# Column order of a gated product, and split loads of a grouped attention's values

## The chip, the cores and the metric

The kernel runs on one core of one Trainium2 chip: TensorE multiplies matrices, VectorE, ScalarE and GpSimd work elementwise, SyncE issues transfers, and 16 DMA engines move data between HBM and SBUF. The metric is device time in microseconds (us) of one execution; lower is better. The profile shows one execution, and its times count from the first instruction.

## The reference

Attention of two kinds is added, and the sum, one row of 512 for each of 8 x 576 = 4608 tokens, goes through a gated product and two further matrices. The inputs are float32 (the weights arrive as 64-bit words that the kernel joins itself).

```python
B, H, S, D = 8, 8, 576, 64
q_d, k_d, v_d = (x.reshape(B, H, S // 4, 4, D).mean(axis=3) for x in (q, k, v))
out_up = np.repeat(sm_attn(q_d, k_d, v_d), 4, axis=2)          # pooled attention, 144 positions
scores = np.where(abs(pos[:, None] - pos[None, :]) < 4, scale * q @ k.T, -1e9)
out_local = softmax(scores) @ v                                # each token sees 7 neighbours
x = (out_up + out_local).transpose(0, 2, 1, 3).reshape(4608, 512)
h = ((x @ w1) * (x @ w2)) @ w3                                 # w1, w2: 512 x 1024, w3: 1024 x 1024
return h @ w_out                                               # w_out: 1024 x 512
```

## The kernel before, in words

**Units and chunks.** A batch element has three units of 192 tokens, so there are 24 units. Two units make a chunk of 384 tokens (CT), and 12 chunks, c = 0 to 11, go through the gated product one after the other. w3 and w_out are multiplied once at the start (fold, the accw products), so that a chunk needs the gates (pab) and one product with the folded matrix wphl (acc).

**Local attention** is made in two ways. The first two batch elements (PB, units 0 to 5, chunks 0 to 2) use group_unit: TensorE computes scores of groups of 16 positions, each of four tokens, against the 18 positions around them. Each unit has three groups; load_v fetches the values of 18 positions x 4 tokens as 72 rows of 2 KB into a buffer v_w, of which there are four (BUFS vw). A group that straddles position 72, where the array in HBM has its halves, is fetched in two transfers. group_values (oe_ps) consumes them. The other batch elements (units 6 to 23, chunks 3 to 11) use unit: VectorE, with ScalarE's help, multiplies and adds windows of q, k and v (q_t, kv, pr, pv, xl), with partitions (head, block), where a sequence is cut into NB = 16 blocks of BT = 36 tokens. In such a unit the token columns of x run (token in block, block), so 16 neighbouring columns are one token offset in 16 blocks.

**Pooled attention** (pooled, quad; s_ps, t_ps, o_ps) is computed once per batch element and added to x. Its v sums are made by accumulating transfers that GpSimd issues.

**The gated product.** moe(c) takes x as high and low parts (xh, xl). For each of eight blocks f of 128 features, TensorE makes both gates into PSUM (pab, 24 products of 384 columns); ScalarE copies the first gate (a, L1008); VectorE multiplies the second into it (L1010); ScalarE writes its high part gh (L1015); VectorE subtracts to the low part gl (L1017). There are two buffers each of a, gh and gl. Then TensorE multiplies 128-column slices of gh and gl, as weights, with wphl: nine products of 512 columns for each f (lines 310 to 312, in this order: gh with the high part, gh with the low part, gl with the high part). The three results (acc) are copied to o_sb, 128 tokens each, and stored by SyncE; in the last chunk the middle one is copied by VectorE and issued from ScalarE's queue. A column of gh is a row of o_sb. For chunks 0 to 2 a store is contiguous; from chunk 3 on a tile of 128 rows is 8 token offsets of 16 blocks (or 4 and 4 of two batch elements), and its rows go to HBM through out_v with the token outermost and the block inside.

**Order.** Every task belongs to an engine's queue, and the order on each queue is written out by hand (ORDER); the costs in the code only merge these queues. SyncE's queue mixes all loads and stores in one order, and a store or load that waits for data or a buffer holds what stands behind it.

Of the kernel before, what the change touches and what calls it, by code (L numbers as in the profile page):

```python
# [8 lines left out]
F32 = mybir.dt.float32  # L9
# [5 lines left out]
ALU = mybir.AluOpType  # L15
# [8 lines left out]
NB = 16  # L24
BT = S // NB
NJ = 3
# [4 lines left out]
QB = SD // 2  # L31
# [7 lines left out]
UN = UT * NB  # L39
CT = 2 * UN  # L40
# [3 lines left out]
PB = (0, 1)  # L44
GS = 16
GQ = GS * FAC
WS = GS + 2
# [140 lines left out]
class Plan:  # L188
# [14 lines left out]
    def add(self, eng, cost, fn, deps=(), take=(), uses=(), late=0.0):  # L203

        got, rings, after = [], [], []
        for r in take:
            held, old, last = r.take()
            got.append(held)
            rings.append(old)
            after += last[:1]  # L210
        t = Task(eng, cost, fn, [d for d in deps if d is not None], late, rings, after, self.group)
        for h in list(got) + list(uses):
            h.append(t)
        self.tasks.append(t)
        return (t, *got) if take else t
# [32 lines left out]
def dve_us(n, fast=False):  # L248
    return n / 1920 + 0.155 if fast else n / 960 + 0.1


def act_us(n, pointers=0, psum=False):
    return n / 1200 + (0.08 if psum else 0.1 if pointers else 0.145) + 0.093 * pointers - (0.03 if psum and pointers else 0.0)
# [6 lines left out]
def mm_us(n):  # L260
    return n * 0.43e-3 + 0.0095
# [5 lines left out]
def dma_us(n, add=False, rate=300e3):  # L267
    return n / (180e3 if add else rate)
# [3 lines left out]
def tile_attention_moe(ctx: ExitStack, tc: tile.TileContext, q, kw, vw, qk4, v4, w1, w2, w3, wout, edge, out):  # L272
    nc = tc.nc
# [32 lines left out]
    add = plan.add  # L306
    R = {k: Ring(n) for k, n in BUFS.items()}

    def three(out_ps, lh, ll, rh, rl, first, last):
        nc.tensor.matmul(out_ps, lhsT=lh, rhs=rh, start=first, stop=False)  # L310
        nc.tensor.matmul(out_ps, lhsT=lh, rhs=rl, start=False, stop=False)  # L311
        nc.tensor.matmul(out_ps, lhsT=ll, rhs=rh, start=False, stop=last)  # L312
# [371 lines left out]
    @plan.named  # L684
    def group_unit(n):
        b, j = divmod(n, NJ)
        c, u = divmod(n, 2)
        T = {}
        starts = [(GS * g, min(max(GS * g - 1, 0), SD - WS)) for g in range(NG * j, NG * j + NG)]

        T["v"], lvs, hvs = [None] * NG, [], []
        for g, (_, k0) in enumerate(starts):
            def load_v(g=g, k0=k0):
                T["v"][g] = pools["pep"].tile([GK, H * D], F32, name="v_w", bufs=BUFS["vw"])
                i = k0
                while i < k0 + WS:
                    m = min(k0 + WS, i // QB * QB + QB)
                    nc.sync.dma_start(out=T["v"][g][FAC * (i - k0):FAC * (m - k0)], in_=v4[b, :, i % QB:i % QB + m - i, i // QB].rearrange("f j h d -> j f (h d)"))
                    i = m
            lv, hv = add("SP", 0.55 * (1 + (k0 < QB < k0 + WS)), load_v, take=[R["vw"]], late=dma_us(GK * 2048))  # L700
            lvs.append(lv)
            hvs.append(hv)
        pep.extend(lvs)
        quads = [group_scores(b, j, qd, starts) for qd in range(2)]

        @plan.named
        def rest(n):
            hpt = None
            pts = []
            for qd, (U, hs, no) in enumerate(quads):  # L710
                def flip(U=U):
                    for par in range(2):
                        U["t", par] = ps.tile([GK, NG, 2 * GQ], F32, tag="g", name="te_ps", bufs=BUFS["ps"])
                        for g in range(NG):
                            nc.tensor.transpose(out=U["t", par][:, g], in_=U["p"][:, par, g], identity=ident)  # L715
                fl, *banks = add("PE", 2 * NG * 0.106, flip, no, take=[R["ps"], R["ps"]], uses=[hs])
                pep.append(fl)
                for par, bank in enumerate(banks):
                    def keep(par=par, U=U, qd=qd):
                        if qd == par == 0:  # L720
                            T["pt"] = pools["pep"].tile([GK, NQ, 2, NG, GQ], F32, name="pte", bufs=BUFS["pte"])
                        nc.scalar.copy(out=T["pt"][:, 2 * qd:2 * qd + 2, par].rearrange("p w g q -> p g w q"), in_=U["t", par].rearrange("p g (w q) -> p g w q", w=2))
                    if hpt is None:
                        th, hpt = add("ACT", act_us(UN * 2, psum=True), keep, [fl], take=[R["pte"]], uses=[bank])
                    else:
                        th = add("ACT", act_us(UN * 2, psum=True), keep, [fl, pts[0]], uses=[bank, hpt])
                    pts.append(th)
            pep.extend(pts)
            group_values(n, T, pts, hpt, lvs, hvs)
        return rest  # L730
# [225 lines left out]

    group = lambda f: 0 if f < 4 else f // 2 - 1
    per = lambda f: 4 if f < 4 else 2
    out_v = out.rearrange("(b k t) m -> b t k m", k=NB, t=BT)

    @plan.named
    def moe(c):
        T = {}
# [22 lines left out]
        for f in range(NF):  # L986
            plan.group = f"gates {c} {f}"
            ends, banks = [], []
            for which in range(2):
                t = None  # L990
                for part in range(2):
                    def mmul(which=which, part=part, f=f):
                        whl, fs = gates[which][group(f)], slice(f % per(f) * 128, f % per(f) * 128 + 128)
                        if part == 0:
                            T["p", which, f] = ps.tile([128, CT], F32, tag="ab", name="pab", bufs=BUFS["ab"])
                        for kk in (2 * part, 2 * part + 1):
                            three(T["p", which, f], whl[:, kk, 0, fs], whl[:, kk, 1, fs], chunks[c][0][:, kk], chunks[c][1][:, kk], kk == 0, kk == KT - 1)
                    d = [t] + x_ready[c] + g_ready[which, group(f)]
                    if part == 0:
                        t, bank = add("PE", 6 * mm_us(CT), mmul, d, take=[R["ab"]], uses=[x_held[c]])  # L1000
                    else:
                        t = add("PE", 6 * mm_us(CT), mmul, d, uses=[x_held[c], bank])
                ends.append(t)
                banks.append(bank)

            def copy_a(f=f):
                T["a", f] = work.tile([128, CT], F32, name="a", bufs=BUFS["a"])
                nc.scalar.copy(out=T["a", f], in_=T["p", 0, f])  # L1008
            ta, ha = add("ACT", act_us(CT, psum=True), copy_a, [ends[0]], take=[R["a"]], uses=[banks[0]])
            tg = add("DVE", dve_us(CT), lambda f=f: nc.vector.tensor_tensor(out=T["a", f], in0=T["p", 1, f], in1=T["a", f], op=ALU.mult), [ta, ends[1]], uses=[ha, banks[1]])  # L1010

            def hi(f=f):
                T["gh", f] = work.tile([128, CT], F32R, name="gh", bufs=BUFS["g"])
                T["gl", f] = work.tile([128, CT], F32R, name="gl", bufs=BUFS["g"])
                nc.scalar.copy(out=T["gh", f], in_=T["a", f])  # L1015
            th, hg = add("ACT", act_us(CT), hi, [tg], take=[R["g"]], uses=[ha])
            tl = add("DVE", dve_us(CT), lambda f=f: nc.vector.tensor_tensor(out=T["gl", f], in0=T["a", f], in1=T["gh", f].bitcast(F32), op=ALU.subtract), [th], uses=[ha, hg])  # L1017
            lag.append((f, [th, tl], hg))

        for f, d, hg in lag:  # L1020
# [13 lines left out]
        for i, (t, ho) in enumerate(kept):  # L1034
            def store(i=i):
                lo = i * 128
                queue = nc.scalar if last and i == 1 else nc.sync
                while lo < i * 128 + 128:
                    n = 2 * c + lo // UN
                    b, t = n // NJ, (n % NJ) * UT + lo % UN // NB  # L1040

                    hi = min(i * 128 + 128, lo // UN * UN + UN if b in PB else lo + (BT - t) * NB)
                    o = T["o", i][lo - i * 128:hi - i * 128]
                    if b in PB:
                        nc.sync.dma_start(out=out[c * CT + lo:c * CT + hi], in_=o)
                    else:
                        queue.dma_start(out=out_v[b, t:t + (hi - lo) // NB], in_=o)
                    lo = hi
            add("SP", 0.5, store, [t] + [k for k, _ in kept[2:] if last and i == 1], uses=[ho], late=dma_us(128 * 2048))

# [128 lines left out]
```

## Time and profile before

| | |
|---|---|
| time, median of 3 runs | 756.76 us (755.49 to 761.6) |
| the profiled execution | 758.0 us, span 756.2 us from first to last instruction |
| granted TensorE clock, mean | 0.995 of 2.4 GHz |
| busy: TensorE products | 741.5 us (98%) |
| busy: VectorE, ScalarE, GpSimd | 608.0 (80%), 534.8 (71%), 128.4 us (17%) |
| moved by DMA | 111.89 MB, mean 148 GB/s |

Busy times are shares of the whole span; what a change in one stage is worth must be read from that stage. Matmuls are pipelined, so a busy TensorE says that products follow one another, not how long one takes. Issuing a transfer is not counted as busy time.

### The profile page before, as it was taken

The numbers are of one execution on the slowest core, as the hardware profiler recorded it, in microseconds if no ns is written. First come the engines' busy times: TensorE is split into PE (matmuls) and PEld (weight loads), VectorE is DVE, ScalarE is ACT, GpSimd is POOL, SyncE is SP. The second block draws the span as 40 slices with busy tenths as digits, with TensorE's granted clock in tenths as the row PEclk, the third lists the DMA queues.
The fourth block names the chain that finished last, engine by engine and source line by source line (L and its number), as shares of the span: only waits on it lengthen the run. The fifth ranks groups of instructions, "written<-read, shape, count | busy, mean of one in ns | idle before, by whom it ended". The sixth has DMA issues, their size and how long they took to land.

```text
span 756.2 us, 14865 instructions
## 1 busy us (share of the span) xinstructions
PE 741.5 (98%) x5288; PEld 646.5 (85%) x5288; DVE 608.0 (80%) x1063; ACT 534.8 (71%) x2133; POOL 128.4 (17%) x163
## 2 busy tenths in 40 slices
PE   7999999999999999999999999999999999999995
PEld 5445798889989999999998998999989898999995
DVE  4867995649999999999899989999988897866111
ACT  4689878658987887797687786887786876762211
POOL 2120013220202321222131220223100222010000
PEclk9999999999999999999999999999999999999998
DMA  8998666646766777657865866577754556232101
GB/s 297 303 233 274 218 199 116 136 88 188 133 171 172 162 165 187 138 117 152 215 113 167 179 129 149 131 173 148 183 117 126 120 117 146 60 68 43 41 1 42
DMA packets 51462, 111.89 MB, mean 148 GB/s; under 512 B 5548, under 2 KB 19884, under 8 KB 51388
## 3 DMA queue, kind: packets, MB, share of 16 engines
q0 software_dynamic: 15360, 38.94, 30.9%
q1 hardware_dynamic: 35892, 71.75, 29.5%
q8 instruction: 41, 0.67, 0.4%
q14 instruction: 33, 0.27, 0.1%
q10 hardware_dynamic: 136, 0.26, 0.1%
HBM read 80.26 MB, written 9.44 MB: 119 GB/s over the span
## 4 chain that ended last, share of the span: by engine, by line
PE 93%; DMA 4%; DVE 1%; ACT 1%; issue 0%; SPq 0%; DVEq 0%; ACTq 0%
PE pab L310 18%; PE pab L312 18%; PE pab L311 18%; PE acc L310 9%; PE acc L311 9%; PE acc L312 9%; PE accw L414 4%; DMA raw<-in_w_dram 4%; PE o_ps L529 2%; PE t_ps L607 2%; PE s_ps L568 2%; PE oe_ps L788 1%; PE se_ps L745 1%; PE te_ps L715 1%; DMA v_w<-in_v_dram 1%
## 5 line engine op out<-in xcount | busy, mean ns | idle before, releaser
L918 ACT ACTIVATE pv<-kv,s 128x64 f32<-128x64 f32 x432 | 115.2, 338 | 14.4 <-DVE s L895 9.1
L870 ACT ACTIVATE junk<-pr 128x64 f32<-128x64 f32 x432 | 110.4, 256 | 17.3 <-DVE pr L860 7.8
L860 DVE TENSOR_TENSOR pr<-q_t,kv 128x768 f32<-128x768 f32 x126 | 116.5, 951 | 1.7 <-ACT junk L870 0.9
L310 PE MATMUL acc<-wphl,gh 128*128 128x512 f32 x288 | 114.1, 396 | 0.0
L312 PE MATMUL acc<-wphl,gl 128*128 128x512 f32 x288 | 112.9, 392 | 0.0
L311 PE MATMUL acc<-wphl,gh 128*128 128x512 f32 x288 | 112.8, 392 | 0.0
L934 POOL DMA_DIRECT2D xl<-pv x54 | 49.3, 912 | 321.2 <-DVE xl L936 263.8
L1010 DVE TENSOR_TENSOR a<-pab,a 128x384 f32<-128x384 f32 x96 | 53.0, 553 | 53.4 <-PE pab L312 52.5
L1008 ACT COPY a<-pab 128x384 f32<-128x384 f32 x96 | 45.2, 471 | 59.0 <-PE pab L312 51.8
L873 DVE TENSOR_REDUCE s<-pr 128x12 f32<-128x768 f32 x90 | 84.3, 946 | 0.3
L870 ACT ACTIVATION_READ_ACCUMULATOR junk<-pr 128x1 f32 x432 | 81.2, 188 | 0.0
L1015 ACT CAST gh<-a 128x384 fp32r<-128x384 f32 x96 | 48.4, 508 | 42.2 <-PE acc L311 29.7
L926 DVE TENSOR_TENSOR pv<-kv,s 128x768 f32<-128x768 f32 x72 | 67.8, 951 | 1.8 <-DMA xl<-pv 1.2
L310 PE MATMUL pab<-xh,wb 128*128 128x384 f32 x192 | 66.1, 344 | 0.0
L310 PE MATMUL pab<-xh,w1a 128*128 128x384 f32 x192 | 65.7, 342 | 0.0
L310 PE MATMUL pab<-xh,wo 128*128 128x384 f32 x192 | 65.3, 340 | 0.0
L312 PE MATMUL pab<-xh,wb 128*128 128x384 f32 x192 | 65.1, 339 | 0.0
L311 PE MATMUL pab<-xl,wb 128*128 128x384 f32 x192 | 65.0, 339 | 0.0
L310 PE MATMUL pab<-xh,w2a 128*128 128x384 f32 x192 | 64.9, 338 | 0.0
L312 PE MATMUL pab<-xh,wo 128*128 128x384 f32 x192 | 64.5, 336 | 0.0
L312 PE MATMUL pab<-xh,w1a 128*128 128x384 f32 x192 | 64.5, 336 | 0.0
L311 PE MATMUL pab<-xl,w1a 128*128 128x384 f32 x192 | 64.4, 336 | 0.0
(120 smaller groups left out, 1716.7 us busy)
## 6 DMA issues: line engine op xcount, KB each, us to landing
xl<-pv POOLq DMA_DIRECT2D x54, 384.0 KB, 4.3
raw<-in_w_dram SPq DMA_DIRECT2D x32, 512.0 KB
qks<-in_qk_dram POOLq DMA_DIRECT2D x18, 576.0 KB, 7.3
kv<-in_kw_dram SPq DMA_DIRECT2D x18, 576.0 KB
kv<-in_vw_dram SPq DMA_DIRECT2D x18, 576.0 KB
out_dram<-o_sb SPq DMA_DIRECT2D x29, 256.0 KB
q_t<-in_q_dram SPq DMA_DIRECT2D x18, 384.0 KB
raw<-in_wout_dram SPq DMA_DIRECT2D x8, 512.0 KB
```

Source lines behind the costliest of these rows:

```text
L310: nc.tensor.matmul(out_ps, lhsT=lh, rhs=rh, start=first, stop=False)
L311: nc.tensor.matmul(out_ps, lhsT=lh, rhs=rl, start=False, stop=False)
L312: nc.tensor.matmul(out_ps, lhsT=ll, rhs=rh, start=False, stop=last)
L860: (nc.gpsimd if o in share["qk_pool"] else nc.vector).tensor_tensor(out=T[o], in0=T["q"], in1=T["k"][:, o * D:o * D + nq].rearrange("p (t ...
L870: nc.scalar.activation(out=junk, in_=T[o][:, t], func=AF.Copy, accum_out=T["s"][:, t, o:o + 1])
L873: reds.append(add("DVE", dve_us(nq), lambda o=o: nc.vector.tensor_reduce(out=T["s"][:, :, o], in_=T[o], op=ALU.add, axis=AX.X), [tp], uses ...
L918: nc.scalar.mul(out=T["pv", o][:, tt], in_=T["v"][:, (tt + o) * D:(tt + o + 1) * D], mul=T["s"][:, tt, o:o + 1])
L926: nc.vector.tensor_tensor(out=T["pv", o], in0=T["v"][:, o * D:o * D + nq].rearrange("p (t d) -> p t d", d=D), in1=T["s"][:, :, o].unsqueez ...
L934: t = add("Pool", 0.9, lambda o=o: nc.gpsimd.dma_start(out=T["x"], in_=T["pv", o], accum_op=ALU.add), [t, tm], uses=[hx, h], late=dma_us(1 ...
L1008: nc.scalar.copy(out=T["a", f], in_=T["p", 0, f])
L1010: tg = add("DVE", dve_us(CT), lambda f=f: nc.vector.tensor_tensor(out=T["a", f], in0=T["p", 1, f], in1=T["a", f], op=ALU.mult), [ta, ends[ ...
L1015: nc.scalar.copy(out=T["gh", f], in_=T["a", f])
```

## The change

In load_v, a group's 18 positions are fetched as a transfer of 16 positions and one of 2 (16 of the 18 groups; the two that straddle the halves stay two transfers of 9). In moe, from chunk 3 on (runs_of gives 0 before), gh and gl are written with their columns turned: within each run of r tokens (r = 8, and 4 in chunks 4, 7 and 10, where a chunk holds two batch elements) the order (token, block) becomes (block, token). The copy to gh writes through the turned view, and the subtraction writes gl and reads gh through it; a is read as before. The stores follow: a run of r tokens goes to HBM with the 16 blocks outermost and its r tokens, neighbouring rows, inside. In chunks 4, 7 and 10 each tile of 128 rows holds two runs, hence two stores. Orders, buffers and costs stay the same.

```diff
--- before.py
+++ after.py
@@ -694,7 +694,7 @@
                 T["v"][g] = pools["pep"].tile([GK, H * D], F32, name="v_w", bufs=BUFS["vw"])
                 i = k0
                 while i < k0 + WS:
-                    m = min(k0 + WS, i // QB * QB + QB)
+                    m = min(k0 + WS if i > k0 else k0 + GS, i // QB * QB + QB)
                     nc.sync.dma_start(out=T["v"][g][FAC * (i - k0):FAC * (m - k0)], in_=v4[b, :, i % QB:i % QB + m - i, i // QB].rearrange("f j h d -> j f (h d)"))
                     i = m
             lv, hv = add("SP", 0.55 * (1 + (k0 < QB < k0 + WS)), load_v, take=[R["vw"]], late=dma_us(GK * 2048))
@@ -956,7 +956,20 @@
 
     group = lambda f: 0 if f < 4 else f // 2 - 1
     per = lambda f: 4 if f < 4 else 2
-    out_v = out.rearrange("(b k t) m -> b t k m", k=NB, t=BT)
+    out_v = out.rearrange("(b k t) m -> b k t m", k=NB, t=BT)
+    out_t = out.rearrange("(b k t) m -> b t k m", k=NB, t=BT)
+
+
+    def runs_of(c):
+        if any(n // NJ in PB for n in (2 * c, 2 * c + 1)):
+            return 0
+        return 8 if (2 * c + 1) % NJ else 4
+
+    def by_block(x, c, turned):
+        r = runs_of(c)
+        if not r:
+            return x
+        return x.rearrange("p (i k t) -> p i t k" if turned else "p (i t k) -> p i t k", k=NB, t=r)
 
     @plan.named
     def moe(c):
@@ -1012,9 +1025,9 @@
             def hi(f=f):
                 T["gh", f] = work.tile([128, CT], F32R, name="gh", bufs=BUFS["g"])
                 T["gl", f] = work.tile([128, CT], F32R, name="gl", bufs=BUFS["g"])
-                nc.scalar.copy(out=T["gh", f], in_=T["a", f])
+                nc.scalar.copy(out=by_block(T["gh", f], c, True), in_=by_block(T["a", f], c, False))
             th, hg = add("ACT", act_us(CT), hi, [tg], take=[R["g"]], uses=[ha])
-            tl = add("DVE", dve_us(CT), lambda f=f: nc.vector.tensor_tensor(out=T["gl", f], in0=T["a", f], in1=T["gh", f].bitcast(F32), op=ALU.subtract), [th], uses=[ha, hg])
+            tl = add("DVE", dve_us(CT), lambda f=f: nc.vector.tensor_tensor(out=by_block(T["gl", f], c, True), in0=by_block(T["a", f], c, False), in1=by_block(T["gh", f], c, True).bitcast(F32), op=ALU.subtract), [th], uses=[ha, hg])
             lag.append((f, [th, tl], hg))
 
         for f, d, hg in lag:
@@ -1038,13 +1051,14 @@
                 while lo < i * 128 + 128:
                     n = 2 * c + lo // UN
                     b, t = n // NJ, (n % NJ) * UT + lo % UN // NB
-
-                    hi = min(i * 128 + 128, lo // UN * UN + UN if b in PB else lo + (BT - t) * NB)
+                    r = runs_of(c)
+
+                    hi = min(i * 128 + 128, lo // UN * UN + UN if n // NJ in PB else lo + (r or BT - t) * NB)
                     o = T["o", i][lo - i * 128:hi - i * 128]
-                    if b in PB:
+                    if n // NJ in PB:
                         nc.sync.dma_start(out=out[c * CT + lo:c * CT + hi], in_=o)
                     else:
-                        queue.dma_start(out=out_v[b, t:t + (hi - lo) // NB], in_=o)
+                        queue.dma_start(out=out_v[b, :, t:t + r] if r else out_t[b, t:t + (hi - lo) // NB], in_=o)
                     lo = hi
             add("SP", 0.5, store, [t] + [k for k, _ in kept[2:] if last and i == 1], uses=[ho], late=dma_us(128 * 2048))
 
```

## Rows read from the trace of the kernel before

**Rows 1.** Windows: stretch, length, busy us of each engine, TensorE's clock, DMA share, GB/s.

```profile
200.00:600.00 400.00, 400.00 (x2595) 366.51 (x2594) 374.79 (x583) 314.66 (x1374) 81.14 (x95) 1.00 0.67 152
...
638.30:645.00 6.70, 6.70 (x56) 6.17 (x41) 3.32 (x5) 4.07 (x13) 0.00 (x0) 0.75 0.42 135
```

**Rows 2.** Chain that ended last, whole span: by line; a piece (start, us, what).

```profile
by line: PE pab L310 18.3%; PE pab L312 17.7%; PE pab L311 17.6%; PE acc L310 8.8%; PE acc L311 8.7%; PE acc L312 8.7%; PE accw L414 4.1%; DMA raw<-in_w_dram 3.6%; PE o_ps L529 2.0%; PE t_ps L607 1.7%; PE s_ps L568 1.7%; PE oe_ps L788 1.2%;
...
635.39 1.73 issue
```

**Rows 3.** Timeline 745 to 757: start, us, engine, line, operation [idle before, releaser].

```profile
747.75 1.97 SPq L1047 DMA_DIRECT2D out_dram<-o_sb  x2
...
748.50 0.58 ACT L1031 COPY o_sb<-acc 128x512 f32<-128x512 f32 x1 [0.77 <-PE acc L312]
748.54 1.22 ACTq L1047 DMA_DIRECT2D out_dram<-o_sb  x1
```

**Rows 4.** Windows of the last microseconds, columns as in rows 1.

```profile
749.00:750.00 1.00, 0.00 (x0) 0.00 (x0) 0.00 (x0) 0.08 (x1) 0.00 (x0) 1.00 0.54 61
750.00:751.00 1.00, 0.00 (x0) 0.00 (x0) 0.00 (x0) 0.00 (x0) 0.00 (x0) 1.00 0.44 154
...
752.00:753.00 1.00, 0.00 (x0) 0.00 (x0) 0.00 (x0) 0.00 (x0) 0.00 (x0) 0.50 0.52 197
...
754.00:755.00 1.00, 0.00 (x0) 0.00 (x0) 0.00 (x0) 0.00 (x0) 0.00 (x0) 0.50 0.09 31
```

**Rows 5.** DMA view 697 to 703, GB/s in 40 slices: one store alone.

```profile
GB/s 0 0 0 0 0 0 0 0 0 0 0 0 0 0 68 109 55 55 27 27 55 41 96 205 164 164 205 218 164 82 14 0 0 0 0 0 0 0 0 0
```

**Rows 6.** DMA view 216 to 222, GB/s in 40 slices: a contiguous store comes first.

```profile
GB/s 0 0 0 0 0 0 0 0 0 137 410 410 410 314 164 259 177 177 178 246 218 191 178 273 154 92 0 184 307 338 338 430 430 369 430 399 270 0 0 0
```

**Rows 7.** Timeline 153 to 164: v_w's last loads and the product that waits.

```profile
155.91 2.08 SPq L698 DMA_DIRECT2D v_w<-in_v_dram  x2
...
161.66 1.16 PEld L788 LDWEIGHTS oe_ps<-pte,v_w 72*32 72x32 f32 x80 [0.40 <-DMA v_w<-in_v_dram]
161.66 1.32 PE L788 MATMUL oe_ps<-pte,v_w 72*32 72x64 f32 x80 [0.24 <-DMA v_w<-in_v_dram]
```

**Rows 8.** Chain that ended last, 155 to 163: the load's piece.

```profile
156.83 4.79 DMA v_w<-in_v_dram
```

**Rows 9.** Issues of lines 698 and 1047: ns min/median/max, first and last start.

```profile
L698 SPq DMA_DIRECT2D v_w<-in_v_dram x20: 754/764/1156, 56.9 to 156.8; - x20
...
L1047 SPq DMA_DIRECT2D out_dram<-o_sb x29: 543/610/1005, 324.0 to 749.1; - x29
```

**Rows 10.** SyncE's waits: line, releaser, us in total, times, longest.

```profile
SPq L842 <- DVE pv L926: 105.4, 7, 27.7
```

**Rows 11.** Groups by form: out<-in, shapes, count | busy us, mean ns | idle before.

```profile
L1017 DVE TENSOR_TENSOR gl<-a,gh 128x384 fp32r<-128x384 f32 x96 | 52.6, 552 | 14.4 <-ACT gh L1015 14.1
...
L1015 ACT CAST gh<-a 128x384 fp32r<-128x384 f32 x96 | 48.4, 508 | 42.2 <-PE acc L311 29.7 <-DVE a L1010 9.3 <-DVE gl L1017 1.5
...
L954 DVE TENSOR_TENSOR xl<-xt,xh 128x768 fp32r<-128x768 f32 x18 | 17.1, 953 | 2.5 <-ACT xh L953 2.5
...
L342 ACT ACTIVATE w<-raw 128x512 f32<-128x512 f32 x16 | 11.1, 703 | 4.2 <-DMA raw<-in_w_dram 4.1
...
L648 DVE COPY qn<-q 128x576 f32<-128x576 f32 x8 | 5.1, 654 | 0.0
...
L467 ACT CAST w1a<-wx 128x512 fp32r<-128x512 f32 x4 | 2.5, 617 | 0.3 <-DVE wx L357 0.3
```

**Rows 12.** Timeline 693 to 697: gl of a chunk's last feature block, and its products.

```profile
695.61 0.55 DVE L1017 TENSOR_TENSOR gl<-a,gh 128x384 fp32r<-128x384 f32 x1
...
696.47 0.39 PE L310 MATMUL acc<-wphl,gh 128*128 128x512 f32 x1
...
696.92 0.39 PE L312 MATMUL acc<-wphl,gl 128*128 128x512 f32 x1
```

**Rows 13.** Timeline 589 to 592.6: a chunk's last x, and its first gate product.

```profile
590.41 0.96 DVE L954 TENSOR_TENSOR xl<-xt,xh 128x768 fp32r<-128x768 f32 x1 [0.90 <-ACT xh L953]
...
592.27 0.44 PE L310 MATMUL pab<-xh,w1a 128*128 128x384 f32 x1
```

## The prediction

> **What bounds the kernel now.** I read busy time by stage, then the chain that ended last, then the end of the timeline, then each place that the change touches. Between 200 and 600 us TensorE is busy for all of the 400 us at full clock, VectorE for 374.79 and ScalarE for 314.66 [rows 1]. The chain says the same: three lines of matmuls on two tiles, six entries, make 80% of the span [rows 2]. So a microsecond counts in two ways only: TensorE is made to wait (or stops waiting), or something lies behind its last matmul. VectorE is the next candidate: it idles 25.2 us in those 400, and what it is given more is hidden only while that lasts. One wait of TensorE is left late in the run, 1.73 us at 635.39, ahead of the pooled values' products; what it waited for the chain doesn't name [rows 2]. Behind it the granted clock is 0.75 between 638.3 and 645 [rows 1]: half of those 6.7 us at 1.2 and not 2.4 GHz, a loss of 1.7 us.
>
> The end: the last chunk's stores are issued by SyncE, the first at 747.75 and the last at 749.1, behind ScalarE's last copy (748.50, for 0.58), and by ScalarE's queue at 748.54, which takes 1.22 [rows 3, 9]. From 749 on nothing but these three stores of 256 KB moves, with a busy share of the transfer engines of 0.44 to 0.54 and, once all are under way, 154 to 197 GB/s; the last microsecond with data has 31 GB/s, 0.2 us at that rate, so data ends at 754.2 [rows 4], 2.0 us ahead of the span's end. A busy share near one half fits a store spread over eight of sixteen engines. These 5 us hold the run's only exposed stores.
>
> **Part 1, stores by block.** From chunk 3 on the token columns in gh and gl are put in the order (block, token), so that a store's slowest dimension in memory is 16 blocks and not 8 or 4 tokens. Two rows price a store of 256 KB. The one of the stretch from 697, in the old shape, moves its data in 17 slices of 0.15 us, 2.5 us, slow for the first 1.2 us and then at up to 218 GB/s [rows 5]. The first burst from 216, a contiguous store, has 137, three times 410 and 314 GB/s, 252 KB in 0.7 us [rows 6]. The new shape writes 8 neighbouring rows for each block and then jumps, so it is nearer to the second, but it may start slowly like the first. At the end the second and third store start their data at about 750.1 (the issue on ScalarE's queue ends at 749.76, and 749 to 750 has only 61 GB/s [rows 4]). Both at 410 GB/s need 1.3 us, to 751.4; at 2.5 us together, to 752.6. With the same 2.0 us behind, the end moves from 756.2 to 753.4 or 754.6: a gain of 1.6 to 2.8. I take 2.3, on the side of the contiguous row. The earlier stores are waited for by nobody on the path: cost and gain nothing. In chunks 4, 7 and 10 each tile is stored in two pieces where two of the three went in one: 6 more issues of 0.61 us [rows 9]. Behind them on SyncE stand the loads of q, k and v for VectorE's units; SyncE itself waits for buffers there (105.4 us in 7 waits at one line [rows 10]), which covers them. Without that cover: 3.6 us.
>
> **Part 2, the turned columns.** gh (ScalarE) and gl (VectorE) are written with a step of 32 bytes (16 in chunks 4, 7, 10) between neighbouring elements instead of 4, and gl's subtraction reads gh with that step too. 72 of 96 instructions of each kind change; TensorE reads both contiguously as before. Now they take 508 and 552 ns for 384 elements [rows 11]. No row has a write with such a step. The nearest are reads: VectorE's copy of 576 elements with a step of 576 bytes takes 654 [rows 11]; its slope from 384 to 768 contiguous elements is (953 - 552)/384 = 1.04 ns, so the elements alone are 599, and at a doubled price they would be near 1200. On ScalarE, 512 elements read with a step of 8 bytes take 703, contiguous ones 617 [rows 11] (the function differs too): 0.17 ns an element. So I take VectorE +0 and ScalarE +65 ns for 384 elements. Bounds: nothing, and the element time doubled, 384 x 1.04 = 400 ns on VectorE and, with the slope (617 - 508)/128 = 0.85, 327 on ScalarE. A gain is excluded: as many instructions on as many elements.
>
> [...]
>
> Where does a price go? Gates and down-products are staggered, and there is a margin from gl's end to the product that needs it. It is smallest in the last feature block of a chunk: gl starts at 695.61 and takes 0.55, the block's first product starts at 696.47, the one that reads gl 0.45 later [rows 12]. So 0.3 to 0.75 us stand against 0.065 expected, and 0.33 or 0.73 at the bounds. The other way is VectorE's pace: a chunk's last x is ready at 591.37, TensorE's first product with it starts at 592.27 [rows 13]. If VectorE loses ScalarE's 65 ns in each of 8 waits for gh, that is 0.5 us a chunk, inside these 0.9. For what gets through, mainly the wait at 635 growing, I put down 0.4 us.
>
> **Part 3, v of a group as 16 and 2 positions.** 16 of the 18 group loads become two transfers (two straddle the halves and stay two of 9). An issue takes 764 ns in the median, a store's 610 [rows 9], so 16 more cost SyncE 10 to 12 us, spread from 57 to 157 us. Behind them stand weight loads and the next v. The place that decides is the last unit: two loads are issued from 155.91 on, back to back, when TensorE has freed their buffers [rows 7]. The one at 156.83 takes 4.79 us to land [rows 8], and for it TensorE starts 0.24 late at 161.66, its weight load 0.40 [rows 7]. Four issues take the place of two, and the last 2 positions go out at about 155.91 + 3 x 0.8 = 158.3. A piece of a ninth of the size may land in 3 us, at 161.3, which ends the wait of 0.40, or in the same 4.79, at 163.1, 1.4 later than now. I take +0.2, nearer to the short end, since the piece is small.
>
> [...]
>
> **The sum.** -2.3 + 0.4 + 0.2 = -1.7. The profiled execution took 758.0 (span 756.2, and 1.8 around it), so 756.3; the median of the three runs is 1.24 lower, 756.76, so 755.1 against it.
>
> **The rivals.** (a) Writes at the doubled price on both engines. VectorE gets 72 x 0.4 = 29 us more. Chunks 3 to 9 lie in the stretch of 400 us: 56 x 0.4 = 22 us against 25.2 idle, of which I let half be usable, since the rest is waiting for matmuls, gh and transfers that stays. The 10 us left over, and 2 or 3 more from chunk 10 and from waits for a later gh, come onto TensorE through x: +12, 767, slower. It decides from about 0.2 us more per gl. For it stand VectorE's pace and the margin of 0.9; against it the 654 ns. [...] (b) ScalarE alone doubles: 24 us on an engine with 85 idle in the 400; VectorE waits longer for gh and the smallest margins break: +1 to +3, 757. (c) The last v comes 1.4 late and the clock falls behind it as at 638: 1.4 + 1.7 in place of 0.2, 758.0. (d) The stores are no faster, since memory or issue and not the number of engines sets their pace (the slow first 1.2 us of [rows 5] speak for it, the busy share of one half [rows 4] against): 757.4. (e) The wait at 635 and its clock go, because transfers ahead of it shift: -3.4, 751.7.
>
> **How the numbers follow.** The forecast (by the bounds of its terms 753.6 to 757) 0.65; (a) 0.08; (b) 0.10; (c) 0.06; (d) 0.07; (e) 0.04. 1% is 7.6 us, about what a measurement of this kernel can tell from no change (the runs lie from 755.49 to 761.6). Only (a) passes it upward; below it there is no case, and 0.02 is left for what I haven't seen: faster 0.02, same 0.90, slower 0.08. The range takes in the forecast, (b), (c) and (d) with some spread of runs, and stops at (e): 752.0 to 759.5.
>
> **What would show it.** Right: over 300 GB/s behind 749 with a busy share near 1, the last data before 753, a span near 754.5; gl at 552 ns, gh between 508 and 600; no new wait of TensorE. Wrong: gl over 750 or gh over 800 ns, and TensorE waiting for x or gl in chunks 3 to 10; a wait for v near 161 of over 1 us with a lower clock behind it; last stores still at a half share.

## The result, and the profile after

The changed kernel took 763.82 us (median of 6 runs, 763.22 to 768.29) against 757.07 for the kernel before (6 runs on the same chip, 754.68 to 761.6): ratio 1.0102 with a 95% interval of 1.0062 to 1.0141. (Ratios here and below are those on record, computed over the runs; they are not the quotient of the two medians.) That is slower by about 1%, outside the range of 752.0 to 759.5, and the wrong way from 755.1. The profiled execution took 763.33, with a span of 761.5 against 756.2.

The costliest groups by form first (columns as in [rows 11]; these lines answer to gh and gl there, 508 and 552 ns; idle is the engine's idle time before them and what ended it):

```profile
L1028 ACT CAST gh<-a 128x384 fp32r<-128x384 f32 x96 | 78.9, 829 | 35.5 <-PE acc L311 19.8 <-DVE a L1023 9.4 <-DVE pr L860 3.3
L1030 DVE TENSOR_TENSOR gl<-a,gh 128x384 fp32r<-128x384 f32 x96 | 78.7, 823 | 18.8 <-ACT gh L1028 18.3
```

Both are means over the 24 contiguous instructions of chunks 0 to 2 and the 72 turned ones. By the view of one tile, the eight gl and gh of chunk 3 (a step of 32 bytes between written elements) and then of chunk 4 (16 bytes) take, in ns, min/median/max:

```profile
L1030 DVE TENSOR_TENSOR gl<-a,gh x8: 859/960/1017, 275.8 to 320.8; 128x384 fp32r<-128x384 f32 x8
L1028 ACT CAST gh<-a x8: 929/982/1107, 274.5 to 319.8; 128x384 fp32r<-128x384 f32 x8
...
L1030 DVE TENSOR_TENSOR gl<-a,gh x8: 837/858/870, 332.5 to 373.2; 128x384 fp32r<-128x384 f32 x8
L1028 ACT CAST gh<-a x8: 866/884/891, 330.8 to 372.3; 128x384 fp32r<-128x384 f32 x8
```

The median of the 32-byte step is 408 ns over the 552 that gl took before: the "element time doubled", 400 ns, that stood in the prediction as a bound. gh has 474 more, beyond its bound of 327. Over all six chunks with this step the medians are 939 and 959 (+387 and +451), and single instructions spread from 850 to 1107.

What TensorE does with that, in the timeline of the end of chunk 5 (start, us, engine, line, operation, idle before and its releaser):

```profile
429.49 0.55 DVE L1023 TENSOR_TENSOR a<-pab,a 128x384 f32<-128x384 f32 x1
...
430.13 0.94 ACT L1028 CAST gh<-a 128x384 fp32r<-128x384 f32 x1 [1.02 <-DVE a L1023]
...
431.11 0.93 DVE L1030 TENSOR_TENSOR gl<-a,gh 128x384 fp32r<-128x384 f32 x1 [0.20 <-ACT gh L1028]
...
431.13 0.19 PEld L310 LDWEIGHTS acc<-wphl,gh 128*128 128x128 f32 x1 [0.26 <-ACT gh L1028]
...
432.09 0.19 PEld L312 LDWEIGHTS acc<-wphl,gl 128*128 128x128 f32 x1 [0.67 <-DVE gl L1030]
432.10 0.50 PE L312 MATMUL acc<-wphl,gl 128*128 128x512 f32 x1 [0.23 <-DVE gl L1030]
```

The weight load of the product with gh sat idle for 0.26 us until gh ended, that of the product with gl for 0.67 until gl ended at 432.04. The two prices lie one behind the other, a, then gh, then gl, where the last feature block of a chunk had 0.3 to 0.75 us to spare [rows 12]. The chain that ended last, by line, says it of the whole span:

```profile
by line: issue 13.7%; PE pab L310 8.8%; PE pab L312 8.4%; PE pab L311 8.4%; DVE pr L860 5.1%; PE acc L310 4.0%; PE acc L312 3.9%; PE acc L311 3.8%; PE accw L414 3.6%; DVE s L873 3.3%; DVE gl L1030 3.1%; DMA xl<-pv 2.6%; ACT junk L870 2.3%;
```

TensorE's six lines fall from 80% [rows 2] to 37%, and VectorE's own work (pr, s, gl) is in it. (The 13.7% called issue is time in which the engine waited for nothing that the profile shows.)

Waits of TensorE, and of its weight loads (us in total, times, longest); in the trace of before only one of them has a counterpart, the weight loads' wait for a, with 0.3 in one wait:

```profile
PE pab L310 <- DVE a L1023: 1.5, 4, 0.6
PE acc L312 <- DVE gl L1030: 1.2, 3, 0.7
...
PE pab L310 <- ACT a L1021: 0.8, 2, 0.5
```

```profile
PEld acc L312 <- DVE gl L1030: 4.9, 8, 1.1
...
PEld pab L310 <- DVE a L1023: 3.9, 7, 1.0
```

The weight loads tell more than the matmuls, whose modelled ends cover short delays (0.23 idle against 0.67 at 432.1 above): the idle time before the five loads that can wait here (L312 acc, and L310 for wb, wo, w1a and w2a) adds up to 19.9 us before and 30.6 after. The largest of the five, before and after (busy, mean ns, idle before):

```profile
L312 PEld LDWEIGHTS acc<-wphl,gl 128*128 128x128 f32 x288 | 54.0, 188 | 11.7
...
L312 PEld LDWEIGHTS acc<-wphl,gl 128*128 128x128 f32 x288 | 54.0, 188 | 16.3 <-DVE gl L1030 4.9
```

Besides gl itself, TensorE waits for a, which frees the gate's bank (pab) and comes late because ScalarE and VectorE do. No line names x.

The windows of the stretch of [rows 1] and of the tail (columns as there):

```profile
200.00:600.00 400.00, 396.90 (x2549) 357.67 (x2548) 383.19 (x573) 322.98 (x1348) 78.52 (x91) 1.00 0.66 150
```

```profile
756.00:757.00 1.00, 0.25 (x2) 0.00 (x0) 0.30 (x1) 0.59 (x1) 0.00 (x0) 1.00 0.26 57
757.00:758.00 1.00, 0.00 (x0) 0.00 (x0) 0.00 (x0) 0.00 (x0) 0.00 (x0) 1.00 0.83 231
758.00:759.00 1.00, 0.00 (x0) 0.00 (x0) 0.00 (x0) 0.00 (x0) 0.00 (x0) 1.00 0.88 254
759.00:760.00 1.00, 0.00 (x0) 0.00 (x0) 0.00 (x0) 0.00 (x0) 0.00 (x0) 1.00 0.78 242
```

In the same 400 us the trace has 46 products fewer than in [rows 1], 2549 and 2595 (a few records can be missing from a trace). The last stores now move 231 to 254 GB/s at a share of 0.78 to 0.88, where [rows 4] has 61 to 197 at about one half; and the last issue on ScalarE's queue takes 0.66 instead of 1.22:

```profile
755.54 1.90 SPq L1061 DMA_DIRECT2D out_dram<-o_sb  x2
...
755.86 0.39 PE L312 MATMUL acc<-wphl,gl 128*128 128x512 f32 x1
756.29 0.59 ACT L1044 COPY o_sb<-acc 128x512 f32<-128x512 f32 x1 [0.77 <-PE acc L312]
756.33 0.66 ACTq L1061 DMA_DIRECT2D out_dram<-o_sb  x1
```

The account of the span: chunk 3 starts (first product of w1a) at 267.68 instead of 269.42, -1.74; from there to the start of the last product 488.18 instead of 478.65, +9.53; from there to the end 5.64 instead of 8.13, -2.49. Sum +5.30, which is 761.5 - 756.2.

By chunk, from one chunk's first product to the next one's (us; the last to its last product's start). The three right columns are runs of the next section.

| chunk | written step | before | after | gl alone (dve_only) | gh alone (act_only) | padded_short |
|---|---|---|---|---|---|---|
| 3 | 32 bytes | 53.71 | +2.13 | +0.87 | +0.19 | +1.86 |
| 4 | 16 | 52.85 | +0.51 | +0.20 | 0.00 | +2.77 |
| 5 | 32 | 54.94 | +2.01 | +1.02 | -0.02 | +3.49 |
| 6 | 32 | 53.93 | +0.57 | +0.30 | 0.00 | +0.57 |
| 7 | 16 | 51.63 | +1.08 | +0.54 | 0.00 | +1.50 |
| 8 | 32 | 55.80 | +1.76 | +1.22 | +1.23 | +1.90 |
| 9 | 32 | 56.32 | +1.35 | +2.09 | -0.22 | +1.76 |
| 10 | 16 | 49.92 | +0.15 | +0.12 | +0.10 | +0.22 |
| 11 | 32 | 49.56 | -0.02 | -0.02 | 0.00 | 0.00 |

Chunk 9 holds the wait at 635 of the kernel before and its half clock [rows 1, 2] (0.50 from 639 to 642, where products of 384 columns start 0.32 us apart, against 0.17 or 0.18 at 699 with a clock of 1.00), and chunk 8 is 1.19 longer in split_only too, which turns nothing; copy_plain, below, which changes nothing near chunk 9, is 1.30 shorter there. These two lines are less sure. In chunks 3 to 7, which have neither, the change costs 6.30 us. The last chunk costs nothing. Each column is one profiled execution.

### The profile page after: what moved, and what is told of

Same layout as the page of the kernel before. It is cut to its first block, busy times and chain, and to the rows that moved or that the text cites. A ratio compares the mean times of both kernels' runs of the same rounds, so it can differ in the third digit from the quotient of the medians.

```text
span 761.5 us, 14897 instructions
## 1 busy us (share of the span) xinstructions
PE 746.9 (98%) x5288; PEld 644.6 (85%) x5288; DVE 632.6 (83%) x1063; ACT 558.2 (73%) x2133; POOL 128.8 (17%) x163
## 3 DMA queue, kind: packets, MB, share of 16 engines
q0 software_dynamic: 15360, 38.94, 30.6%
## 4 chain that ended last, share of the span: by engine, by line
PE 47%; DVE 22%; issue 14%; ACT 8%; DMA 6%; POOL 3%; SPq 0%; DVEq 0%; POOLq 0%; ACTq 0%
PE pab L310 9%; PE pab L312 8%; PE pab L311 8%; DVE pr L860 5%; PE acc L310 4%; PE acc L312 4%; PE acc L311 4%; PE accw L414 4%; DVE s L873 3%; DVE gl L1030 3%; DMA xl<-pv 3%; ACT junk L870 2%; DVE pv L926 2%; DVE xl L936 2%; DMA raw<-in_wout_dram 2%
## 5 line engine op out<-in xcount | busy, mean ns | idle before, releaser
L312 PE MATMUL acc<-wphl,gl 128*128 128x512 f32 x288 | 113.8, 395 | 1.5 <-DVE gl L1030 1.2
L310 PE MATMUL acc<-wphl,gh 128*128 128x512 f32 x288 | 114.3, 397 | 0.0
L1028 ACT CAST gh<-a 128x384 fp32r<-128x384 f32 x96 | 78.9, 829 | 35.5 <-PE acc L311 19.8
L1030 DVE TENSOR_TENSOR gl<-a,gh 128x384 fp32r<-128x384 f32 x96 | 78.7, 823 | 18.8 <-ACT gh L1028 18.3
L312 PEld LDWEIGHTS acc<-wphl,gl 128*128 128x128 f32 x288 | 54.0, 188 | 16.3 <-DVE gl L1030 4.9
L310 PE MATMUL pab<-xh,wb 128*128 128x384 f32 x192 | 65.8, 343 | 0.6 <-DVE a L1023 0.4
L310 PE MATMUL pab<-xh,w2a 128*128 128x384 f32 x192 | 65.3, 340 | 1.1 <-DVE a L1023 1.1
L310 PE MATMUL pab<-xh,wo 128*128 128x384 f32 x192 | 65.7, 342 | 0.6 <-ACT a L1021 0.5
L310 PE MATMUL pab<-xh,w1a 128*128 128x384 f32 x192 | 65.8, 343 | 0.0
L312 PE MATMUL pab<-xh,wb 128*128 128x384 f32 x192 | 64.6, 336 | 0.0
L312 PE MATMUL pab<-xh,wo 128*128 128x384 f32 x192 | 64.5, 336 | 0.0
```

The source lines that it names most:

```text
L1028: nc.scalar.copy(out=by_block(T["gh", f], c, True), in_=by_block(T["a", f], c, False))
```

## The experiments

The diffs are against the changed kernel, or against the kernel before where the text says "in the kernel before". Ratios are against the kernel before on the same chip.

**split_only.** Part 3 alone, in the kernel before.

```diff
-                    m = min(k0 + WS, i // QB * QB + QB)
+                    m = min(k0 + WS if i > k0 else k0 + GS, i // QB * QB + QB)
```

> Part 3 alone: v of a group as 16 and 2 positions; columns and stores as before. Theory A (the loss is the doubled time of gh's and gl's writes): gh 508 and gl 552 ns as before, no loss, and the time is 757 less what the split itself gives. Of that there are two readings: the changed kernel started chunk 2 (TensorE's first product with w1a) 1.75 us earlier than before; if the split did that, the time is 755.3 and chunk 2 starts near 212.7; if it is scatter of the start-up, the time is 756.5 to 757.5. The wait of TensorE for v near 161 (0.24, its weight load 0.40) is gone in both. Rival B (longer queue on SyncE delays loads): the 16 more issues cost something here already, 758 or more.

758.33 against 756.43, ratio 1.0013 (0.9988 to 1.0037); gh 508 and gl 550 ns. Chunk 3 starts at 267.51, 1.9 earlier than in the trace of before, but chunk 8 takes 1.19 and chunk 9 1.01 more, and the lead is gone; TensorE's waits hold the one ahead of the pooled values' products (o_ps) once more, and one for gl:

```profile
PE o_ps L529 <- issue: 2.3, 1, 2.3
...
PE acc L312 <- DVE gl L1017: 0.6, 1, 0.6
```

The median lies where the longer queue was expected to put it (758 or more), but the interval takes in 1. So the slowdown is not part 3's, and whether part 3 alone gains or costs a little the runs can't tell.

**block_only.** Parts 1 and 2 alone: the line above put back in the changed kernel.

> Parts 1 and 2 alone: turned columns and stores by block; v of a group loaded as 18 positions, as before. Theory A: gh 830 and gl 825 ns in the mean of 96 (near 935 and 915 in the 72 that are turned), TensorE loses 8 to 10 us between chunk 3 and the last chunk, the tail is 2.5 us shorter: 763.5 to 765.5, as the changed kernel or above it by the split's gain of at most 1.7. If the split were to blame for a part: below 762.5.

765.41 against 756.43, 1.0104 (1.0064 to 1.0144); gh 829, gl 826. From chunk 3's start to the last product 490.10, 11.5 over before. The whole slowdown lies in the turned columns and the stores by block.

**read_side.** The same order of columns, made by reading with a step (64 bytes) and writing contiguously, so that the 16 blocks are an outer dimension and the run of 8 or 4 tokens is the innermost one.

```diff
+    def by_run(x, c, turned):
+        r = runs_of(c)
+        if not r:
+            return x
+        return x.rearrange("p (i k t) -> p i k t" if turned else "p (i t k) -> p i k t", k=NB, t=r)
...
-                nc.scalar.copy(out=by_block(T["gh", f], c, True), in_=by_block(T["a", f], c, False))
+                nc.scalar.copy(out=by_run(T["gh", f], c, True), in_=by_run(T["a", f], c, False))
```

and gl in the same way.

> As the changed kernel, but the turn lies on the side of the read: ScalarE and VectorE write gh and gl contiguously, in the order (block, token), and read a with a step of 64 bytes; stores by block and split loads stay. Theory A in its narrow form (only a write with a far step is dear; the copy of 576 elements read with a step of 576 bytes was not): gh 508, gl 552 ns, no loss up to the last chunk, and the shorter tail stays: 753 to 755. In its wide form (any operand with a far step costs the same): gh near 935, gl near 915, 763 to 765. Rival B (the loss comes from the stores by block, which occupy all 16 engines, and from the longer queue of SyncE): gh and gl short and still 762 or more.

761.25, 1.0066 (1.0037 to 1.0095). The groups by form:

```profile
L1034 ACT CAST gh<-a 128x384 fp32r<-128x384 f32 x96 | 74.5, 780 | 36.9 <-PE acc L311 23.5 <-DVE a L1029 8.7 <-DVE s L880 2.8
L1036 DVE TENSOR_TENSOR gl<-a,gh 128x384 fp32r<-128x384 f32 x96 | 72.6, 758 | 18.5 <-ACT gh L1034 17.7
```

In the turned chunks that is 871 and 827 ns. The price is not one of writes alone: one operand read with a far step brings two thirds (gl) and three quarters (gh) of that of the 32-byte writes. The time lies between what the two forms of the expectation gave, 753 to 755 and 763 to 765. The reading copy that the prediction went by must hide something; copy_plain, below, looks at that.

**last_only.** The turned columns and the stores by block in the last chunk alone, v as in the changed kernel.

```diff
     def runs_of(c):
-        if any(n // NJ in PB for n in (2 * c, 2 * c + 1)):
+        if c < NC - 1:
             return 0
```

> Turned columns and stores by block in the last chunk only (8 of 96 instructions of each kind); split loads stay. Theory A: the 2.5 us of the tail without the loss: 753.5 to 755, chunk 11's gates and products as long as before, because nothing but gh and gl is left for ScalarE and VectorE there. If the tail's gain depended on the stores before it (engines free of them): 756.5 or more.

755.77, 0.998 (0.9957 to 1.0003). From the last product's start (748.17) to the end of the span (753.6) 5.4 us, the short tail of the changed kernel; gh and gl in this one chunk at 953 and 948 ns hurt nothing, as the last line of the table says of the changed kernel too: with no attention unit left beside it VectorE has the room (in the changed kernel it is busy for 12 of the last chunk's 50 us). The median is above the 753.5 to 755 that were expected, and nothing here says why.

**act_only.** gl written contiguously, gh turned.

```diff
-            tl = add("DVE", dve_us(CT), lambda f=f: nc.vector.tensor_tensor(out=by_block(T["gl", f], c, True), in0=by_block(T["a", f], c, False), in1=by_block(T["gh", f], c, True).bitcast(F32), op=ALU.subtract), [th], uses=[ha, hg])
+            tl = add("DVE", dve_us(CT), lambda f=f: nc.vector.tensor_tensor(out=T["gl", f], in0=T["a", f], in1=T["gh", f].bitcast(F32), op=ALU.subtract), [th], uses=[ha, hg])
```

> As the changed kernel, but gl is made by the subtraction of before, all operands contiguous, so that gl's columns no longer match gh's (the output mixes low parts of other columns); ScalarE's write of gh stays turned. It takes ScalarE's price alone: gh 829 ns in the mean, gl 552. If what binds is VectorE's time (it was busy for 375 of 400 us before), little is lost in the middle: 2 to 3 us, less the tail's 2.5, so 756 to 758. If what binds is the length of the way from gate to product (gh, then gl, then the product), half of the loss of 9.5 us stays: 759 to 760.5.

756.86 against 755.93, 1.0001 (0.9984 to 1.0017); gh 827, gl 552. In chunks 3 to 7 of its trace it loses 0.17 us: there ScalarE's 430 ns more fit in. This kernel keeps the stores by block and the split loads, so neither of these costs anything in those chunks. The ten runs as a whole are less clear: the tail is 2.5 us shorter and the time is not, so about 2.5 us is lost elsewhere on average, and the profiled run, 754.69, is the fastest of the ten.

**dve_only.** gh copied contiguously, gl turned. (The text on record says that the output mixes columns. It doesn't: gl holds what turned a is over this gh, so their sum is still the turned product.)

```diff
-                nc.scalar.copy(out=by_block(T["gh", f], c, True), in_=by_block(T["a", f], c, False))
+                nc.scalar.copy(out=T["gh", f], in_=T["a", f])
```

> As the changed kernel, but gh is the contiguous copy of before, so its columns are not turned (the output mixes columns); VectorE's subtraction keeps the turned write of gl and the turned read of gh. It takes VectorE's price alone: gh 508, gl 823 ns in the mean. If VectorE's time binds: most of the loss stays, 760 to 763. If the way from gate to product binds: about half, 759 to 760.5.

759.5, 1.0052 (1.0031 to 1.0074); gh 508, gl 823. In chunks 3 to 7 it loses 2.93 us. So VectorE's price is the one that hurts by itself, but the two alone, 2.93 and 0.17, are half of the 6.30 of both. That is what a margin would do: gh's 0.43 us fits into it, gl's 0.4 in part, both in a row don't. It rests on one execution of each in five chunks. By the ratios, with the 2.5 us of the tail added back, about 2.5 us is lost by act_only, 6.4 by dve_only and 10.2 by the changed kernel, so that the two alone make up most of the loss; whether two prices cost more than their sum is not shown.

**step8.** Runs of 2 tokens, so that written elements lie 8 bytes apart; the stores are then smaller.

```diff
-        return 8 if (2 * c + 1) % NJ else 4
+        return 2
```

> As the changed kernel, with runs of 2 tokens and not 8 or 4: neighbouring elements of gh and gl lie 8 bytes apart, in instructions with as many dimensions and the same 16 elements in the innermost; a tile of 128 rows is stored in four pieces of 32 rows. [...] If any step other than one element, or the pattern with three dimensions itself, costs: gh near 935 and gl near 915 in the 72, 829 and 823 in the mean, as with steps of 32 and 16 bytes.

A single run, 757.35:

```profile
L1030 DVE TENSOR_TENSOR gl<-a,gh 128x384 fp32r<-128x384 f32 x96 | 52.7, 552 | 15.0 <-ACT gh L1028 14.5
L1028 ACT CAST gh<-a 128x384 fp32r<-128x384 f32 x96 | 51.0, 535 | 41.6 <-PE acc L311 31.3 <-DVE a L1023 10.0
```

VectorE's price is gone and ScalarE's is 37 ns (545 in turned chunks). Chunks 3 to 7 differ from before by -0.01, 0.00, -0.28, 0.00 and 0.00 us. So a step of 8 bytes costs VectorE nothing here (552 ns) and ScalarE little; steps of 16 and 32 bytes cost both (VectorE 306 and 387 ns, ScalarE 376 and 451, by the medians over all chunks in the changed kernel). With the order of columns, the stores by block and the split loads all kept, the loss in these chunks goes with the price. Where between 8 and 16 bytes the price begins, and why, no run shows.

**copy_plain.** In the kernel before, the copy that was the prediction's witness, written and read contiguously.

```diff
-                    nc.vector.tensor_copy(out=fours[b][qd][0][:, w], in_=x["q"].rearrange("p f s -> p s f"))
+                    nc.vector.tensor_copy(out=fours[b][qd][0][:, w].rearrange("p s f -> p (s f)"), in_=x["q"].rearrange("p f s -> p (f s)"))
```

> The kernel before, with one edit in pooled_sums: VectorE's copy of 576 elements reads its source in the order in which it lies, and not with a step of 576 bytes (so the grouped scores get q in another order). It prices the row on which the forecast of VectorE's price rested, 654 ns. If a far read had been free there, as the forecast had it: 650 again. If the row hid a price because a copy of contiguous float32 runs at more than one element a cycle: about 455, as the copy of 512 elements of 16 partitions in this kernel (418) has it with 0.52 ns for each of 64 more and the rest fixed.

A single run, 756.65:

```profile
L648 DVE COPY qn<-q 128x576 f32<-128x576 f32 x8 | 3.4, 451 | 0.0
```

451 ns, not 654. The witness did pay: 203 ns, 0.35 for each element. It looked free because it was held against the subtraction's slope of 1.04 ns an element, and a contiguous float32 copy on VectorE is faster than that: 451 ns for 576 elements, 0.78 for each in all. The trace of before already had one, 512 elements on 16 partitions:

```profile
L511 DVE COPY vl<-vl 16x512 f32<-16x512 f32 x2 | 0.8, 418 | 0.5 <-DMA vl<-in_v_dram 0.5
```

From 418 to 451 that is 0.52 ns for each of 64 elements more, though on 16 partitions there and 128 here; against the subtraction's 1.04 it is half. How long a cycle is, of which the expectation speaks, no run shows.

**padded.** In the kernel before: everything contiguous and the old stores, but from chunk 3 on gh is copied twice and 272 columns of gl are subtracted once more, for a price of the change's size without a step.

```diff
-                nc.scalar.copy(out=T["gh", f], in_=T["a", f])
+                for _ in range(2 if c > 2 else 1):
+                    nc.scalar.copy(out=T["gh", f], in_=T["a", f])
...
+            def low(f=f):
+                for n in (272, CT)[c < 3:]:
+                    nc.vector.tensor_tensor(out=T["gl", f][:, :n], in0=T["a", f][:, :n], in1=T["gh", f][:, :n].bitcast(F32), op=ALU.subtract)
```

> The kernel before, contiguous, with its old stores and loads, but from chunk 3 on gh is copied twice (ScalarE about 0.38 us more) and the first 272 columns of gl are subtracted once more ahead of the whole (VectorE about 0.36 us more): the length of the turned writes without any far step. If the loss of the changed kernel is the length of these 144 instructions alone: chunk 3 to the last product takes 9 to 11 us longer than before, as in the changed kernel, and there is no shorter tail: 764.5 to 767. If the far steps also hurt what runs beside them (other engines' or TensorE's accesses to the same memory): less than half of that, under 761.

779.78 against 757.17, 1.0308 (1.0281 to 1.0335). The extra gl takes 437 ns beside 556, so the pads were too long (764.5 to 767 had been expected for the length alone); the direction agrees and the size says little. Hence the next.

**padded_short.** The same with 256 columns of gh and 160 of gl.

> As the padded kernel, with shorter additions: in that one the pair of gl took 1.03 us and the pair of gh 1.05, against 0.91 and 0.94 of the turned writes. Here 256 columns of gh and 160 columns of gl are done once more: pairs of about 0.93 and 0.91, as the turned writes, all contiguous. If the length alone is the loss: from the first gate product of chunk 4's predecessor (chunk 3) to the last product 8 to 12 us longer than the 478.7 of before, and 764.5 to 768.5 in the median with the old tail. If far steps hurt others besides: under 762. If issuing one more instruction costs by itself (the padded kernel lost 22 us there for additions a third longer than the turned writes): 772 or more.

771.23 against 756.33, 1.0206 (1.0182 to 1.023), above what length alone was given. One pair of each in the timeline:

```profile
405.10 0.94 ACT L1016 CAST gh<-a 128x256 fp32r<-128x256 f32 x2
...
406.26 0.91 DVE L1021 TENSOR_TENSOR gl<-a,gh 128x160 fp32r<-128x160 f32 x2
```

From the start of the first to the end of the second, the gap of some 32 ns between them included, a pair takes 947 and 913 ns (medians). That is as long as the turned writes of 32 bytes, 959 and 939, but some 60 longer than those of 16 bytes, 887 and 858, and here chunks 4, 7 and 10 have the long pairs too. Chunks 3 to 7 lose 10.2 us and not 6.3, by waits of the same kinds. Of the difference 2.7 us lies in chunks 4 and 7, where the pairs are longer; in chunks 3, 6 and 8 the loss is that of the changed kernel within 0.3 us (1.86, 0.57 and 1.90 against 2.13, 0.57 and 1.76); chunk 5, with 1.5 more, stays open. So longer instructions without any far step slow the kernel by as much, and nothing asks for a further harm of the turned writes to others.

**last_nosplit.** last_only with the line of split_only put back: the best of both.

> Turned columns and stores by block in the last chunk only, v of a group loaded as before: the part of the change that gains, without the others. The tail is 2.5 us shorter and gh and gl are dear in 8 instructions of each kind only: 2 to 2.5 us under the kernel before in its median, 753.5 to 754.5, ratio 0.997. If the gain were lost to later starts in the last chunk: 756.

753.01 (12 runs, 751.22 to 757.75) against 757.17, 0.9954 (0.9935 to 0.9973): faster than both kernels. Span 751.2: chunk 3 to last product 477.13 (-1.52, of which chunk 9, the one with the half clock before, has -1.32), start -0.87, tail 5.52 (-2.61). Only the last part is certainly the edit's: copy_plain has the shorter chunk 9 too. The windows of its tail:

```profile
746.00:747.00 1.00, 0.07 (x1) 0.00 (x0) 0.12 (x1) 0.59 (x1) 0.00 (x0) 1.00 0.43 86
747.00:748.00 1.00, 0.00 (x0) 0.00 (x0) 0.00 (x0) 0.00 (x0) 0.00 (x0) 1.00 0.82 248
748.00:749.00 1.00, 0.00 (x0) 0.00 (x0) 0.00 (x0) 0.00 (x0) 0.00 (x0) 1.00 0.92 274
```

## Why the prediction was wrong, step by step

**What bounds the kernel: right.** TensorE's time counted, and VectorE was the next candidate. Its 25.2 us of idle time in the 400 did not shield TensorE: 16.8 of them are still there after, so they lie elsewhere than where TensorE waits for gl or a.

**Part 1, the tail: right, its size in part by luck.** -2.3 forecast, -2.49 measured, -2.61 in last_nosplit. The way there differed: 231 to 254 GB/s and not over 300, and the issue on ScalarE's queue became 0.56 shorter, which had not been forecast; how much of the 2.49 comes from it no run separates. The prediction also took data to end at 754.2, from a rate. In finer slices of the view (before: 748 to 756, 0.2 us each; after: 756 to 762, 0.15 us each) it ends at about 754.7 and 760.0, both 1.5 us ahead of the span's end:

```profile
GB/s 0 0 0 0 0 133 41 51 20 61 51 143 184 174 215 184 205 164 154 143 195 174 215 195 205 195 215 195 215 92 72 41 20 20 0 0 0 0 0 0
...
GB/s 0 0 0 0 55 177 177 177 191 232 355 314 178 219 273 300 300 178 246 246 300 246 259 314 287 178 41 0 0 0 0 0 0 0 0 0 0 0 0 0
```

The eight of sixteen engines were an estimate from the share; measured are the shares, 0.44 to 0.54 before [rows 4] and 0.78 to 0.88 after. The six more issues cost nothing visible (act_only has them, and 0.00 in chunks 4 and 7).

**Part 2, the turned columns: the step that failed.** "So I take VectorE +0 and ScalarE +65 ns" was the sentence; measured at the 32-byte step are about +390 and +450, at 16 bytes +306 and +376 (medians). Two things were wrong in its working. The witness was another operation, and its price was hidden by comparing a copy with the slope of a subtraction; copy_plain shows the contiguous copy at 451. And ScalarE's row of 703 against 617 had a step of 8 bytes; step8 shows that step as nearly free (0 and 37 ns), where 16 bytes cost 306 and 376, so its 0.17 ns an element could not be carried to 32 bytes. With the prices the margins failed too: at its bounds the prediction had put both prices together, 0.73 us, against the 0.75 ahead of the product that reads gl, and gh's came out above its bound, so that they are 0.84 together at 32 bytes. The margin of one block was no measure for all either: VectorE's price alone, 0.4 of those 0.75, still cost 2.93 us in chunks 3 to 7 (dve_only), partly through a wait that the prediction didn't look at, TensorE's for a and the gates' banks. The term of 0.4 us became 9.53 between chunk 3 and the last product.

**Rival (a) is what came,** at a chance of 0.08, +12 there and +9.5 here. The price was about as supposed there (0.4 us for each gl; 0.39 measured at 32 bytes, 0.31 at 16), the way was not: it came onto TensorE through gl and through a's freeing of the gates' banks, not through x, so that the sizes lie so near is luck. (Its 56 instructions in the stretch to 600 us count chunk 9, which starts at 592.27 [rows 13]; 48 are in it.) Rival (b), ScalarE alone, is not what happened, as gl grew too; act_only shows none of its +1 to +3 in chunks 3 to 7, and its ten runs don't exclude it. (d) was refuted by the tail's rate. (c) didn't come: TensorE has no wait for v in the changed kernel. Of (e) half came: the wait at the pooled values' products is there again, 2.3 us at 644.93, but the granted clock behind it is 1.00 from 646 to 660.

**Part 3: no loss or gain that the runs can tell.** The v loads are now 36 issues, and TensorE's wait of 0.24 for v is gone in the changed kernel and in split_only. That it is part 3's doing is not shown: last_only and act_only, which have part 3 too, have one of 0.38 and 0.47, and block_only, which doesn't, has none. Both reach chunk 3 by 1.7 to 1.9 us earlier, but kernels without part 3 start it anywhere from 267.99 (padded_short) to 269.74 (block_only), so the lead may be scatter; the time of split_only, 1.0013, has none of it. The 3 us in which the prediction let a small piece land had no row behind it; in the trace of before, between 153 and 165, GpSimd's transfers of 112 KB took 3.1 us from issue to landing and those of 32 KB 3.7.

**The range** ended at 759.5 because the doubled price was left out of it at 0.08, though it was the upper bound of a term with no direct row; the bounds of 753.6 to 757 left that bound out as well.

## What to carry to other kernels

A row may stand as witness for another instruction only if it is the same operation on the same engine, with its own contiguous twin beside it; a copy that looks free beside another operation's slope may already be paying (654 ns here, 451 contiguous). Add the prices along the chain that feeds the bottleneck before holding them against a margin, and read that margin in more than one place. And where a layout serves an exposed transfer, turn the layout only for that transfer: here the last chunk has all of the tail's gain (2.61 us in last_nosplit) and none of the price.

## What the runs showed of the hardware

- Price of a float32 step on 384 elements (VectorE's subtraction from 552, ScalarE's copy from 508): writes 8 bytes apart 552 and 545 ns (step8); 16 bytes 858 and 884, 32 bytes 960 and 982 (the changed kernel; medians of one chunk; the subtraction reads gh with the same step); reads 64 bytes apart, one operand, 828 and 870 (read_side). Over all chunks the medians are 858 and 887 at 16 bytes, 939 and 959 at 32, so 32 bytes cost some 70 to 80 ns more than 16; at 32 the fastest single subtraction, 850, is as short as those at 16.
- A contiguous float32 copy of 576 elements on VectorE takes 451 ns (copy_plain), 0.78 an element in all, where the subtraction takes 1.04 for each further one [rows 11].
- The issue of a store on ScalarE's queue fell from 1.22 to 0.66 us, and of stores on SyncE in the median from 610 to 544 ns, with the new shape of the stores.
